# Gate and value products one pair ahead, tiles turned one by one, output sums in two halves

## The chip, the cores and the metric

One core of a Trainium2 chip runs the whole program once. The metric is the device time of one execution in microseconds (us). The kernel before took 796.15 us, median of three runs (794.65 to 797.71).

## The reference, cut to what matters

Three layers follow each other on 2304 tokens (4 batches of 576) with 512 features. First a windowed attention, then a mixture of 8 experts with one expert for each token (its result is x), then a gated layer:

```python
gate = 1.0 / (1.0 + np.exp(-(x @ w_gate)))      # w_gate, w_val: 512 x 1536
val = x @ w_val
return (gate * val @ w_out).astype(np.float32)  # w_out: 1536 x 512
```

## The kernel before, in words

The program runs attention, then the experts (`moe_phase`, line 1050), then the gated layer (`moe2_phase`, line 1289). The order of the instructions on every engine's queue is the order in which Python writes them: the schedule is by hand.

**Numbers in two parts.** A float32 operand of the expert's second product and of the gated layer is held as a high and a low part (hi, lo). A product of two such operands is three matmuls: high by high, high by low and low by high (`three`, line 923; `dots`, line 930). ScalarE makes the high part by a cast, VectorE the low part by a subtraction.

**The gated layer.** Its 1536 inner features are 12 chunks f of 128, in 6 pairs q. The tokens are 5 blocks b: block 0 has the tiles of 128 tokens 0 and 1, the blocks 1 to 4 have four tiles each (2 to 5, 6 to 9, 10 to 13, 14 to 17). `s1(f, b)` (line 1326) makes a chunk: `first_products` (line 1278) does the gate and the value product, 12 matmuls each, into two PSUM banks (for block 0 into two halves of one). Then ScalarE takes Tanh (L1341, th), VectorE multiplies (L1342), ScalarE casts the high part (L1345, gh), VectorE subtracts for the low part (L1346, gl). `s2(q, b, parts)` (line 1349) makes the output sums of a block: for every tile six matmuls into one of two banks (6, 7), and the sum is added to `acc` in SBUF, by ScalarE (L1359) at q = 0, by VectorE (L1361, fo) later. At q = 5 SP then stores the tile. `s2` of a block is put (`due`) behind the first `s1` of the next block, all its tiles in a row; for block 0 at q = 0 it stands ahead of block 1, and in the last block of q = 5 behind the second `s1`.

**The first block.** Block 0 is loaded and turned in the expert stage (`xo`, line 1215, `turn_old`, `add_last`, `first_xt`). There half of the products of chunks 0 and 1 are started (lines 1271 and 1274). The tiles 2 to 17 are loaded from DRAM on SP's queue (`load_x`, L1310, tile fx), four ahead, and turned by `make_xt` (line 1313): four transposes on TensorE (L1320), a cast on ScalarE (L1322, fxh), a subtraction on VectorE (L1323, fxl), then the next load. They follow the two chunks of block 0, 1, 2 and 3 at q = 0, two tiles behind each chunk. Tiles 2 and up of DRAM can be read once the last expert's results are scattered (L1084, POOL's queue).

**Weight conversion.** The gated layer's weights lie as 64-bit words in DRAM and are made into float32 parts on the way, in 36 halves of 512 columns (a weight chunk is two halves, a pair has three chunks: gate, value, out). `Convert.tick` (line 1042) moves each of six stages on by at most one half: l loads it raw (SP, L989, cv_raw, 512 KB), o subtracts for the low part (VectorE, L1009), h casts the high part (ScalarE, L1006), c multiplies by the sign (POOL, L999), b rebuilds the number (ScalarE L1032 for the sign, VectorE L1034, L1035, L1038), a takes the absolute value (ScalarE, L994). `until` bounds the casts, so that no part is written over one still in use; five weight chunks have room. In the expert stage `TICKS` says how many ticks follow each expert (11 in all), in the gated layer two ticks follow each chunk of a pair's first block and one each later chunk.

**An expert.** For each of the 8 experts four weight chunks: `products1` (L1157) into one of three banks, then ScalarE (L1202, hh) and VectorE (L1203, hl), `split` of a weight chunk (L919, L920) and `feed` (loads on SP, L910). Then the next expert's tokens are turned (`make_xt` of `moe_phase`), the ticks come, then the second products (L925 to L927), VectorE's `add_up` (L1183), and the scatters on POOL's queue.

Of the kernel before, what the change touches and what calls it, by code (L numbers as in the profile page):

```python
# [8 lines left out]
F32 = mybir.dt.float32  # L9
F32R = mybir.dt.float32r  # L10
BF16 = mybir.dt.bfloat16
I32 = mybir.dt.int32
ACTF = mybir.ActivationFunctionType
ALU = mybir.AluOpType
# [864 lines left out]
class Weights:  # L879
# [4 lines left out]
    N1, N2, NP, NX = 8, 6, 4, 4  # L884
# [38 lines left out]
def three(nc, out, lh, rh, first, last):  # L923

    nc.tensor.matmul(out, lhsT=lh[0], rhs=rh[0], start=first, stop=False)  # L925
    nc.tensor.matmul(out, lhsT=lh[0], rhs=rh[1], start=False, stop=False)  # L926
    nc.tensor.matmul(out, lhsT=lh[1], rhs=rh[0], start=False, stop=last)  # L927


def dots(nc, out, lh, rh, k0, k1, first, last):  # L930

    for k in range(k0, k1):
        for a in range(2):
            nc.tensor.matmul(  # L934
                out, lhsT=lh[a][:, k], rhs=rh[0][:, k], start=first and k + a == k0, stop=False,
                skip_group_check=True,
            )
    for k in range(k0, k1):
        nc.tensor.matmul(  # L939
            out, lhsT=lh[0][:, k], rhs=rh[1][:, k], start=False, stop=last and k == k1 - 1, skip_group_check=True  # L940
        )
# [108 lines left out]
def moe_phase(nc, tc, ctx, g, wt, pool_a, na, route, xd, cv, over, new_xt):  # L1050
# [1 line left out]

    TICKS = (0, 3, 3, 3, 2, 0, 0, 0)
    pool_b = ctx.enter_context(tc.tile_pool(name="m_w", bufs=1, reuse_waits="tile"))
    px = ctx.enter_context(tc.tile_pool(name="m_x", bufs=3, reuse_waits="tile"))
    p = ctx.enter_context(tc.tile_pool(name="m_p", bufs=2, reuse_waits="tile"))
# [30 lines left out]
    def make_xt(e):  # L1089
        xt = p.tile([128, 4, CAP], F32, tag="xt", name="xt")  # L1090

        def turn(h):
            for k in range(4):
                nc.tensor.transpose(xts[h][:, k], xg[e, h][:, 128 * k:128 * k + 128], g.ident)

        turn(0)
        nc.scalar.copy(out=xt[:, :, 0:128], in_=xts[0])
        if e == 0:
            load_n(0)
        with tc.If(taken[e] > 128) as c:  # L1100
            turn(1)
        with c.Else():
            nc.tensor.matmul(xts[1][:, 0, 0:32], lhsT=g.one, rhs=g.one[:, 0:32], start=True, stop=True)
        nc.vector.tensor_copy(xt[:, :, 128:256], xts[1])
        return xt
# [88 lines left out]
    xt = make_xt(0)  # L1194
    for e in range(E):
        hs = []
        for c in range(4):
            ps = g.bank()
            cases(taken[e], lambda n: products1(e, c, n), (128, 144, 160, 192, 256))
            hi = p.tile([128, 2, CAP], F32R, tag="hh", name="hh", bufs=5)  # L1200
            lo = p.tile([128, 2, CAP], F32R, tag="hl", name="hl", bufs=5)
            nc.scalar.activation(out=hi, in_=ps, func=ACTF.Relu)  # L1202
            nc.vector.scalar_tensor_tensor(  # L1203
                out=lo, in0=ps, scalar=0.0, in1=hi.bitcast(F32), op0=ALU.max, op1=ALU.subtract
# [7 lines left out]
            if c == 0 and e == E - 1:  # L1212
# [6 lines left out]
                for h in range(2):  # L1219
                    nc.gpsimd.tensor_scalar(  # L1220
                        out=hot[:, h], in0=route.iota, scalar1=to[:, h:h + 1], scalar2=None, op0=ALU.is_equal
# [3 lines left out]
        if e + 1 < E:  # L1225
            xt = make_xt(e + 1)
        for _ in range(TICKS[e]):
            cv.tick()
# [13 lines left out]
    t = p.tile([128, 4, CAP], F32R, tag="xt", name="part")  # L1242
# [26 lines left out]
    scatter(e, 0)  # L1269
    begun = [(t[:, 0], t[:, 1]) for t in (g.bank(), g.bank())]  # L1270
    first_products(nc, cv, begun[0], xt0, 0, 0, 2)
    add_last(0, 1)
    first_xt(1)
    first_products(nc, cv, begun[1], xt0, 1, 0, 2)
    return xt0, begun


def first_products(nc, cv, ps, xt, f, k0=0, k1=4):


    fs = slice(128 * (f % 2), 128 * (f % 2) + 128)
    shared = xt[0].shape[2] == 256
    for i in range(2):
        whi, wlo = cv.need(3 * (f // 2) + i, 4)
        first = k0 == 0 and (i == 0 or not shared)
        dots(nc, ps[i], (whi[:, :, fs], wlo[:, :, fs]), xt, k0, k1, first, k1 == 4)


def moe2_phase(nc, tc, ctx, g, cv, xt0, begun, acc, xd, out):


    KF = FF // 128
    NP, NB = KF // 2, 5
    tiles = [(0, 1)] + [tuple(range(4 * b - 2, 4 * b + 2)) for b in range(1, NB)]
    p = ctx.enter_context(tc.tile_pool(name="f_p", bufs=2, reuse_waits="tile"))
    px = ctx.enter_context(tc.tile_pool(name="f_xt", bufs=1, reuse_waits="tile"))
    xt = {0: xt0}
    for b in range(1, NB):
        xt[b] = tuple(px.tile([128, 4, 512], F32R, name=f"f{n}{b}") for n in ("xh", "xl"))
    pairs, sums, spares = [(3, 4), (5, 1)], (6, 7), (0, 2)  # L1300
    turn = {"s1": 0, "s2": 0, "x": 0}
    xn = {}

    def bank(i, n=512):
        return g.all[i][:, 0:n]

    def load_x(t):
        if t < NT // 128:
            x = p.tile([128, DM], F32, tag="x", name="fx", bufs=4)
            nc.sync.dma_start(out=x, in_=xd[128 * t:128 * t + 128, :])  # L1310
            xn[t] = x

    def make_xt(t):
        b, a = (t + 2) // 4, (t + 2) % 4
        hi, lo = xt[b]
        x = xn.pop(t)
        turn["x"] += 1
        ps = bank(spares[turn["x"] % 2]).rearrange("p (a c) -> p a c", c=128)
        for k in range(4):
            nc.tensor.transpose(ps[:, k], x[:, 128 * k:128 * k + 128], g.ident)  # L1320
        s = slice(128 * a, 128 * a + 128)
        nc.scalar.copy(out=hi[:, :, s], in_=ps)  # L1322
        nc.vector.tensor_tensor(out=lo[:, :, s], in0=ps, in1=hi[:, :, s].bitcast(F32), op=ALU.subtract)  # L1323
        load_x(t + 4)

    def s1(f, b):
        n = 128 * len(tiles[b])
        k0 = 2 * (b == 0 and f < 2)
        if k0:
            ps = begun[f]  # L1330
        else:
            pair = pairs[turn["s1"] % 2]
            turn["s1"] += 1
            if b == 0:
                ps = bank(pair[0]).rearrange("p (a c) -> p a c", c=256)
                ps = (ps[:, 0], ps[:, 1])
            else:
                ps = (bank(pair[0]), bank(pair[1]))
        first_products(nc, cv, ps, xt[b], f, k0)
        th = p.tile([128, n], F32, tag="th", name="th")  # L1340
        nc.scalar.activation(out=th, in_=ps[0], func=ACTF.Tanh, scale=0.5)  # L1341
        nc.vector.scalar_tensor_tensor(out=th, in0=th, scalar=1.0, in1=ps[1], op0=ALU.add, op1=ALU.mult)  # L1342
        hi = p.tile([128, n], F32R, tag="gh", name="gh", bufs=4)
        lo = p.tile([128, n], F32R, tag="gl", name="gl", bufs=4)
        nc.scalar.copy(out=hi, in_=th)  # L1345
        nc.vector.tensor_tensor(out=lo, in0=th, in1=hi.bitcast(F32), op=ALU.subtract)  # L1346
        return hi, lo

    def s2(q, b, parts):
        whi, wlo = cv.need(3 * q + 2, 2)  # L1350
        for a, t in enumerate(tiles[b]):
            ps = bank(sums[turn["s2"] % 2])
            turn["s2"] += 1
            s = slice(128 * a, 128 * a + 128)
            for i, (hi, lo) in enumerate(parts):
                three(nc, ps, (hi[:, s], lo[:, s]), (whi[:, i], wlo[:, i]), i == 0, i == 1)
            o = acc[t]
            if q == 0:
                nc.scalar.activation(out=o, in_=ps, func=ACTF.Copy, scale=0.5)  # L1359
            else:  # L1360
                nc.vector.scalar_tensor_tensor(out=o, in0=ps, scalar=0.5, in1=o, op0=ALU.mult, op1=ALU.add)  # L1361
            if q == NP - 1:
                nc.sync.dma_start(out=out[128 * t:128 * t + 128, :], in_=o)

    for t in range(2, 6):
        load_x(t)
    after = {(0, 0): (2, 3), (0, 1): (4, 5)}
    for b in range(1, NB - 1):
        after[b, 0], after[b, 1] = tuple(range(4 * b + 2, 4 * b + 4)), tuple(range(4 * b + 4, 4 * b + 6))
    due = None  # L1370
    for q in range(NP):
        order = list(range(NB)) if q < NP - 1 else [1, 2, 3, 4, 0]
        for b in order:
            if (q, b) == (0, 1):
                s2(*due)
                due = None
            parts = []
            last = q == NP - 1 and b == 0
            for i in range(2):
                parts.append(s1(2 * q + i, b))  # L1380
                if q == 0:
                    for t in after.get((b, i), ()):
                        make_xt(t)
                if due and i == last:
                    s2(*due)
                    due = None
                cv.until(2 * min(3 * q + 5, 3 * NP))
                for _ in range(1 + (b == order[0])):
                    cv.tick()
            due = (q, b, parts)  # L1390
    s2(*due)


class Overflow:
# [287 lines left out]
```

## Time and profile before

| what | value |
|---|---|
| median of three runs | 796.15 us (794.65 to 797.71) |
| the profiled execution | 798.2 us |
| its span, first to last instruction | 796.4 us |
| TensorE busy | 739.7 us (93% of the span) |
| VectorE, ScalarE, POOL busy | 421.4, 310.6, 141.1 us |
| mean granted TensorE clock | 0.968 of full speed |
| expert stage, about | 150 to 309.7 us |
| gated layer, about | 309.7 to 796 us |

PE is TensorE's matmuls, PEld its weight loads (which overlap), DVE is VectorE, ACT is ScalarE, SP and POOL are the engines whose queues issue the DMAs. PEclk is the granted clock as a share of the full 2.4 GHz. A matmul's time in a row includes the pipeline's length, so the distance between two starts is its cost. In a timeline row the numbers are the start in us, the length in us, engine, line and operation, output and input by the program's names, the shape and the count; what stands in brackets is how long the engine was idle before it and what ended that. A row by stretch has the stretch, its length, the busy us (and count) of PE, PEld, DVE, ACT and POOL, the granted clock, the mean busy share of the 16 DMA engines and GB/s.

### The profile page before, as it was taken

What the parts mean: (1) busy time and instruction counts of PE and PEld (TensorE: products, weight loads), DVE (VectorE), ACT (ScalarE), POOL (GpSimd) and SP (SyncE); (2) the same over time, 40 slices, a digit from 0 to 9 for tenths busy, and PEclk for the clock granted to TensorE, in tenths of its full rate; (3) what the DMA queues carried; (4) which work ended last, traced back from release to release, by engine and by line L of the source; (5) the groups of instructions that cost most, each with busy time, mean ns of one, the idle gap of its engine ahead of it and who ended that gap; (6) DMA issues with size and microseconds to landing.
All of it is one profiled execution on the core that took longest, in us unless ns stands there. A gap on an engine that the chain in (4) does not pass through costs nothing.

```text
span 796.4 us, 13025 instructions
## 1 busy us (share of the span) xinstructions
PE 739.7 (93%) x4976; PEld 594.0 (75%) x4976; DVE 421.4 (53%) x880; ACT 310.6 (39%) x677; POOL 141.1 (18%) x163
## 2 busy tenths in 40 slices
PE   6989989689998798799999999999999999999995
PEld 3656665478997798677787788778877887777784
DVE  8568677548857564622146336543653473333232
ACT  5887885235544453433253114312431151111110
POOL 7223333312433232200011101100210020000000
PEclk7799999889999999999999999999999999999998
DMA  7779879696697723510002101210220000001112
GB/s 158 170 174 215 219 154 310 183 352 209 201 323 261 271 92 116 181 54 28 0 27 80 53 0 54 67 39 1 56 77 26 1 27 0 1 1 53 54 54 84
DMA packets 74999, 88.13 MB, mean 111 GB/s; under 512 B 15810, under 2 KB 52930, under 8 KB 74912
## 3 DMA queue, kind: packets, MB, share of 16 engines
q1 hardware_dynamic: 71008, 78.68, 34.0%
q0 software_dynamic: 2560, 6.15, 2.3%
q10 hardware_dynamic: 1344, 2.10, 0.7%
q8 instruction: 60, 0.98, 0.5%
q14 instruction: 27, 0.22, 0.1%
HBM read 75.52 MB, written 13.63 MB: 112 GB/s over the span
## 4 chain that ended last, share of the span: by engine, by line
PE 78%; ACT 8%; DVE 6%; DMA 4%; issue 2%; DVEq 0%; SPq 0%; ACTq 0%
PE bank L934 25%; PE bank L939 12%; PE bank L925 9%; PE bank L927 8%; PE bank L926 8%; PE bank L1157 7%; ACT kTd L237 2%; DMA cv_raw<-in_moe_w_out_dram 2%; ACT qTd L237 1%; PE ps_s L255 1%; PE ps_t L221 1%; ACT p L269 1%; ACT kTp L237 1%; ACT xt L386 1%; PE ps_o L302 1%
## 5 line engine op out<-in xcount | busy, mean ns | idle before, releaser
L934 PE MATMUL bank<-fxh,w_hi 128*128 128x512 f32 (+1 forms) x480 | 176.6, 374 | 4.8 <-ACT fxh L1322 4.8
L934 PE MATMUL bank<-fxh,w_lo 128*128 128x512 f32 (+1 forms) x480 | 175.2, 371 | 0.0
L1342 DVE SCALAR_TENSOR_TENSOR th<-th,bank 128x512 f32<-128x512 f32 (+1 forms) x60 | 38.0, 634 | 185.9 <-PE bank L939 168.9
L939 PE MATMUL bank<-fxl,w_hi 128*128 128x512 f32 (+1 forms) x480 | 121.1, 372 | 0.0
L934 PEld LDWEIGHTS bank<-fxh,w_hi 128*128 128x128 f32 x480 | 90.5, 188 | 23.1 <-ACT fxh L1322 5.5
L999 POOL TENSOR_TENSOR cv_x<-cv_x,cv_s 128x512 f32<-128x512 f32 x36 | 48.8, 1357 | 320.2 <-DVE cv_x L1038 320.0
L934 PEld LDWEIGHTS bank<-fxh,w_lo 128*128 128x128 f32 x480 | 90.5, 189 | 16.7
L939 PEld LDWEIGHTS bank<-fxl,w_hi 128*128 128x128 f32 x480 | 85.7, 189 | 17.1
L925 PE MATMUL bank<-w_hi,gh 128*128 128x512 f32 x216 | 87.9, 407 | 5.0 <-ACT gh L1345 4.5
L1341 ACT ACTIVATE th<-bank 128x512 f32<-128x512 f32 (+1 forms) x60 | 33.1, 552 | 146.4 <-PE bank L939 146.4
L1345 ACT CAST gh<-th 128x512 fp32r<-128x512 f32 (+1 forms) x60 | 34.7, 578 | 140.5 <-DVE th L1342 140.5
L927 PE MATMUL bank<-w_hi,gl 128*128 128x512 f32 x216 | 86.0, 398 | 0.0
L926 PE MATMUL bank<-w_lo,gh 128*128 128x512 f32 x216 | 85.9, 397 | 0.0
L1157 PE MATMUL bank<-xt,w 128*128 128x128 f32 (+3 forms) x512 | 72.3, 304 | 13.7 <-issue 8.2
L1157 PEld LDWEIGHTS bank<-xt,w 128*128 128x128 f32 x512 | 70.1, 207 | 16.0 <-issue 9.1
L1361 DVE SCALAR_TENSOR_TENSOR fo<-bank,fo 128x512 f32<-128x512 f32 x90 | 61.7, 688 | 37.0 <-PE bank L927 36.0
L1346 DVE TENSOR_TENSOR gl<-th,gh 128x512 fp32r<-128x512 f32 (+1 forms) x60 | 38.9, 649 | 38.6 <-ACT gh L1345 38.6
L925 PEld LDWEIGHTS bank<-w_hi,gh 128*128 128x128 f32 x216 | 40.9, 189 | 21.4 <-DVE fo L1361 7.6
L927 PEld LDWEIGHTS bank<-w_hi,gl 128*128 128x128 f32 x216 | 41.1, 190 | 10.2 <-DVE gl L1346 0.5
L926 PEld LDWEIGHTS bank<-w_lo,gh 128*128 128x128 f32 x216 | 41.1, 190 | 8.4
L994 ACT ACTIVATE cv_x<-cv_raw 128x512 f32<-128x512 f32 x36 | 24.3, 675 | 57.0 <-issue 24.0
L920 DVE TENSOR_TENSOR w_lo<-w,w_hi 128x1024 fp32r<-128x1024 f32 x32 | 39.1, 1222 | 4.2 <-ACT w_hi L919 4.0
(215 smaller groups left out, 1059.6 us busy)
## 6 DMA issues: line engine op xcount, KB each, us to landing
w<-in_moe_w_dram SPq DMA_DIRECT2D x62, 512.0 KB
cv_raw<-in_moe_w_val_dram SPq DMA_DIRECT2D x12, 512.0 KB
cv_raw<-in_moe_w_out_dram SPq DMA_DIRECT2D x12, 512.0 KB
cv_raw<-in_moe_w_gate_dram SPq DMA_DIRECT2D x10, 512.0 KB
out_dram<-fo SPq DMA_DIRECT2D x18, 256.0 KB
fx<-xd SPq DMA_DIRECT2D x16, 256.0 KB
kp<-in_k_dram SPq DMA_DIRECT2D x12, 192.0 KB
qp<-in_q_dram SPq DMA_DIRECT2D x12, 192.0 KB
```

Of the source, the lines that this page charges most:

```text
L920: self.nc.vector.tensor_tensor(out=lo, in0=raw, in1=hi.bitcast(F32), op=ALU.subtract)
L925: nc.tensor.matmul(out, lhsT=lh[0], rhs=rh[0], start=first, stop=False)
L926: nc.tensor.matmul(out, lhsT=lh[0], rhs=rh[1], start=False, stop=False)
L927: nc.tensor.matmul(out, lhsT=lh[1], rhs=rh[0], start=False, stop=last)
L934: nc.tensor.matmul(out, lhsT=lh[a][:, k], rhs=rh[0][:, k], start=first and k + a == k0, stop=False, skip_group_check=True,)
L939: nc.tensor.matmul(out, lhsT=lh[0][:, k], rhs=rh[1][:, k], start=False, stop=last and k == k1 - 1, skip_group_check=True)
L999: nc.gpsimd.tensor_tensor(out=self.x[i], in0=self.x[i], in1=self.s.pop(i), op=ALU.mult)
L1157: nc.tensor.matmul(ps[:, a, 0:n], lhsT=wt.one[4 * e + c][:, k, 128 * a:128 * a + 128], rhs=xt[:, k, 0:n], start=(k == 0), stop=(k == 3),)
L1342: nc.vector.scalar_tensor_tensor(out=th, in0=th, scalar=1.0, in1=ps[1], op0=ALU.add, op1=ALU.mult)
L1345: nc.scalar.copy(out=hi, in_=th)
L1346: nc.vector.tensor_tensor(out=lo, in0=th, in1=hi.bitcast(F32), op=ALU.subtract)
L1361: nc.vector.scalar_tensor_tensor(out=o, in0=ps, scalar=0.5, in1=o, op0=ALU.mult, op1=ALU.add)
```

## The change

`TICKS` goes from 11 to 15 ticks: one fewer after expert 1, one more after expert 4, two each after experts 5 and 6. With that the first five weight chunks are converted before the gated layer starts. There, the two chunks of pair 1 for block 0 (`ahead`) are computed right behind those of pair 0, before block 0's first sums; they keep their own buffers until pair 1, which then has no block 0 of its own. `make_xt` is called between the gate and the value product of a chunk (`between`), one tile at a time. `s2` becomes a list of one call for each tile (`sums_of`): two sums follow a block's first chunk, the rest the second. At pair 0 there are no ticks until block 3; later pairs have three ticks ahead of their first block and one behind each chunk. The bank pairs change places and th has one buffer.

```diff
-    TICKS = (0, 3, 3, 3, 2, 0, 0, 0)
+    TICKS = (0, 2, 3, 3, 3, 2, 2, 0)
...
-def first_products(nc, cv, ps, xt, f, k0=0, k1=4):
+def first_products(nc, cv, ps, xt, f, k0=0, k1=4, between=None):
...
         dots(nc, ps[i], (whi[:, :, fs], wlo[:, :, fs]), xt, k0, k1, first, k1 == 4)
+        if between:
+            between()
...
-    pairs, sums, spares = [(3, 4), (5, 1)], (6, 7), (0, 2)
+    pairs, sums, spares = [(5, 1), (3, 4)], (6, 7), (0, 2)
     turn = {"s1": 0, "s2": 0, "x": 0}
-    xn = {}
+    xn, todo, due = {}, [], []
...
+    def between():
+        if todo:
+            todo.pop(0)()
...
-        first_products(nc, cv, ps, xt[b], f, k0)
-        th = p.tile([128, n], F32, tag="th", name="th")
+        first_products(nc, cv, ps, xt[b], f, k0, between=None if k0 else between)
+        z, bufs = ("0", 2) if b == 0 and f // 2 == 1 else ("", 4)
+        hi, lo = (p.tile([128, n if z else 512], F32R, tag=t + z, name=t, bufs=bufs)[:, 0:n] for t in ("gh", "gl"))
+        th = p.tile([128, 512], F32, tag="th", name="th", bufs=1)[:, 0:n]
         nc.scalar.activation(out=th, in_=ps[0], func=ACTF.Tanh, scale=0.5)
         nc.vector.scalar_tensor_tensor(out=th, in0=th, scalar=1.0, in1=ps[1], op0=ALU.add, op1=ALU.mult)
-        hi = p.tile([128, n], F32R, tag="gh", name="gh", bufs=4)
-        lo = p.tile([128, n], F32R, tag="gl", name="gl", bufs=4)
...
-    def s2(q, b, parts):
+    def s2(q, a, t, parts):
         whi, wlo = cv.need(3 * q + 2, 2)
-        for a, t in enumerate(tiles[b]):
...
+    def sums_of(q, b, parts):
+        return [lambda a=a, t=t: s2(q, a, t, parts) for a, t in enumerate(tiles[b])]
+
+    def flush(left=0):
+        while len(due) > left:
+            due.pop(0)()
 
     for t in range(2, 6):
         load_x(t)
-    after = {(0, 0): (2, 3), (0, 1): (4, 5)}
-    for b in range(1, NB - 1):
-        after[b, 0], after[b, 1] = tuple(range(4 * b + 2, 4 * b + 4)), tuple(range(4 * b + 4, 4 * b + 6))
-    due = None
+    due += sums_of(0, 0, [s1(0, 0), s1(1, 0)])
+    todo += [lambda: None] + [lambda t=t: make_xt(t) for t in range(2, 6)]
+    ahead = [s1(2, 0), s1(3, 0)]
+    while due:
+        due.pop(0)()
+        between()
     for q in range(NP):
-        order = list(range(NB)) if q < NP - 1 else [1, 2, 3, 4, 0]
+        if q == 1:
+            due += sums_of(1, 0, ahead)
+        order = list(range(1, NB)) if q < 2 else [1, 2, 3, 4, 0] if q == NP - 1 else list(range(NB))
         for b in order:
-            if (q, b) == (0, 1):
-                s2(*due)
-                due = None
+            first = b == order[0]
+            cv.until(2 * min(3 * q + (4 if first else 5), 3 * NP))
+            if q and first:
+                for _ in range(3):
+                    cv.tick()
+            if q == 0 and b < NB - 1:
+                todo += [lambda t=t: make_xt(t) for t in range(4 * b + 2, 4 * b + 6)]
             parts = []
-            last = q == NP - 1 and b == 0
             for i in range(2):
                 parts.append(s1(2 * q + i, b))
-                if q == 0:
-                    for t in after.get((b, i), ()):
-                        make_xt(t)
-                if due and i == last:
-                    s2(*due)
-                    due = None
-                cv.until(2 * min(3 * q + 5, 3 * NP))
-                for _ in range(1 + (b == order[0])):
+                if i and todo:
+                    between()
+                flush(0 if i else 2)
+                if q or b > 2:
                     cv.tick()
-            due = (q, b, parts)
-    s2(*due)
+            due += sums_of(q, b, parts)
+    flush()
```

## Rows read from the trace of the kernel before

**Rows 1.** Busy time by stretch: us, then each engine's busy us (count), clock, DMA.

```profile
309.70:326.66 16.96, 9.74 (x54) 7.76 (x53) 11.58 (x21) 8.80 (x17) 4.07 (x3) 0.90 0.71 226
...
398.83:786.00 387.17, 386.62 (x1760) 313.00 (x1759) 175.27 (x282) 99.47 (x175) 29.53 (x22) 1.00 0.12 37
```

**Rows 2.** Timeline of TensorE, start of the gated layer.

```profile
309.71 0.28 PE L934 MATMUL bank<-fxh,w_hi 128*128 128x256 f32 x1
...
314.03 1.32 PE L1320 MATMUL bank<-ident,fx 128*128 128x128 f32 x8 [2.71 <-DMA fx<-xd]
...
322.83 0.71 PE L925 MATMUL bank<-w_hi,gh 128*128 128x512 f32 x1 [4.49 <-ACT gh L1345]
...
326.66 0.39 PE L934 MATMUL bank<-fxh,w_hi 128*128 128x512 f32 x1
```

**Rows 3.** Chain of waits through the two holes: start, us, what.

```profile
311.29 2.69 DMA fx<-xd
...
316.70 0.60 DVE w_lo L1009
...
322.01 0.34 DVE th L1342
```

**Rows 4.** Chain of waits at block 1's last tiles, and in sums at q = 0.

```profile
338.96 0.70 DVE th L1342
...
340.29 0.98 ACT fxh L1322 x2
...
387.84 0.23 PE bank L925
```

**Rows 5.** Waits from 296 us on: who, for whom, total us, times, longest.

```profile
PEld bank L925 <- DVE fo L1361: 7.6, 16, 0.5
...
PE bank L934 <- ACT fxh L1322: 4.8, 3, 1.6
```

**Rows 6.** Timeline of TensorE behind transposes, and within four sums.

```profile
333.03 0.48 PE L934 MATMUL bank<-fxh,w_hi 128*128 128x512 f32 x1
...
449.33 0.40 PE L927 MATMUL bank<-w_hi,gl 128*128 128x512 f32 x1
449.77 0.50 PE L925 MATMUL bank<-w_hi,gh 128*128 128x512 f32 x1
```

**Rows 7.** Timeline of ScalarE in the expert stage.

```profile
262.27 0.66 ACT L994 ACTIVATE cv_x<-cv_raw 128x512 f32<-128x512 f32 x1 [5.21 <-DMA cv_raw<-in_moe_w_out_dram]
...
283.30 0.60 ACT L1202 ACTIVATE hh<-bank 128x512 fp32r<-128x512 f32 x1 [0.84 <-PE bank L1157]
```

**Rows 8.** Timeline of SP's queue in the expert stage.

```profile
250.20 1.12 SPq L989 DMA_DIRECT2D cv_raw<-in_moe_w_out_dram  x2
...
298.23 1.33 SPq L1215 DMA_DIRECT2D xo<-xd  x2
```

**Rows 9.** Timeline of TensorE in the expert stage.

```profile
241.84 2.44 PE L1157 MATMUL bank<-xt,w 128*128 128x160 f32 x16 [1.96 <-DVE hl L1203]
...
255.57 1.95 PE L1157 MATMUL bank<-xt,w 128*128 128x128 f32 x16
...
264.20 3.16 PE L1157 MATMUL bank<-xt,w 128*128 128x128 f32 x16 [2.07 <-DVE hl L1203]
...
303.36 0.60 PE L1124 MATMUL bank<-ident,xo 128*128 128x128 f32 x4
```

**Rows 10.** Busy time by stretch in the expert stage: columns as in rows 1.

```profile
265.00:270.00 5.00, 5.00 (x26) 4.63 (x25) 5.00 (x7) 4.23 (x6) 1.00 (x1) 0.67 0.57 167
270.00:275.00 5.00, 5.00 (x29) 4.33 (x28) 2.81 (x4) 0.00 (x0) 2.05 (x2) 1.00 1.08 397
```

**Rows 11.** Timeline of VectorE in the expert stage.

```profile
248.63 0.68 DVE L1009 TENSOR_TENSOR w_lo<-cv_x,w_hi 128x512 fp32r<-128x512 f32 x1
...
250.76 0.69 DVE L1009 TENSOR_TENSOR w_lo<-cv_x,w_hi 128x512 fp32r<-128x512 f32 x1
...
288.39 0.74 DVE L1183 SCALAR_TENSOR_TENSOR xg<-bank,r_gslot,xg 128x512 f32<-128x512 f32 x1
```

More of the change, by code (lines that the diff above doesn't have):

```diff
@@ L1347, in s1 @@
         return hi, lo
-    def s2(q, b, parts):
+    def s2(q, a, t, parts):
         whi, wlo = cv.need(3 * q + 2, 2)
-        for a, t in enumerate(tiles[b]):
[L1352 to L1357, printed above, removed]
-            if q == 0:
[L1359 to L1363, printed above, removed]
+        ps = bank(sums[turn["s2"] % 2])
+        turn["s2"] += 1
+        s = slice(128 * a, 128 * a + 128)
+        for i, (hi, lo) in enumerate(parts):
+            three(nc, ps, (hi[:, s], lo[:, s]), (whi[:, i], wlo[:, i]), i == 0, i == 1)
+        o = acc[t]
+        if q == 0:
+            nc.scalar.activation(out=o, in_=ps, func=ACTF.Copy, scale=0.5)
+        else:
+            nc.vector.scalar_tensor_tensor(out=o, in0=ps, scalar=0.5, in1=o, op0=ALU.mult, op1=ALU.add)
+        if q == NP - 1:
+            nc.sync.dma_start(out=out[128 * t:128 * t + 128, :], in_=o)
@@ L1377, in moe2_phase @@
             parts = []
-            last = q == NP - 1 and b == 0
             for i in range(2):
                 parts.append(s1(2 * q + i, b))
-                if q == 0:
-                    for t in after.get((b, i), ()):
-                        make_xt(t)
-                if due and i == last:
-                    s2(*due)
-                    due = None
-                cv.until(2 * min(3 * q + 5, 3 * NP))
-                for _ in range(1 + (b == order[0])):
+                if i and todo:
+                    between()
```

## The prediction, made before the change was built

> **What bounds the kernel now.** I read the busy shares by stage first, then TensorE's timeline for its holes, then the chain of waits through each hole, then the other engines where the change puts work. The reader should see that the second half of the kernel (gate, value and output products, from 309.7 us on) is TensorE's own time with few holes. From 398.83 to 786.00 TensorE is busy 386.62 of 387.17 us at full granted clock, while VectorE is busy 175 and ScalarE 99 [rows 1]: only fewer or shorter holes can shorten this stretch. From 309.70 to 326.66 it is busy 9.74 of 16.96 us at a granted clock of 0.90 [rows 1]. There the holes are.
>
> The first hole, 2.71 us, ends with the load of the first x tile (fx). The second, 4.49 us, ends with ScalarE's gh; behind it the products take 0.71 us instead of about 0.4 [rows 2]. The chain shows why. The x tile cannot be read before the last scatter is done, and lands 2.69 us after its issue. And gh of the second chunk waited for VectorE, which from 316.70 to 322.01 worked only on weight conversions (L1009, L1034 to L1038) queued ahead of L1342 [rows 3]: the order of the program was late there, not the engine.
>
> **The change part by part.** The sum is made against the profiled execution, 798.2 us with a span of 796.4; the median of the three runs shown is 796.15, 2 us lower, and I take the saving off that median.
>
> *Start of the second stage.* A 128x512 product takes 0.23 us from start to start [rows 4], a 128x256 one half of that, 0.12. The stretch from 309.71 to 326.66 [rows 2] holds 24 products of 256 columns (2.9 us), 16 transposes (about 1.6) and 12 products of 512 (2.8): 7.3 of 16.95 us. So 9.6 us are lost. After the change the two chunks of the second pair (48 products of 256, 5.7 us, only moved here from a later place) stand between the first pair and the sums. The first x tile is then wanted at 309.71 + 2.9 + 2.9 = 315.5, 1.5 us after it lands (311.29 + 2.69) [rows 3], and gh of the second chunk only at about 320. With no conversions queued ahead it is ready some 2.2 us after its products: a chain as at 338.96, where L1342 takes 0.70 us and L1345 and L1346 about as long [rows 4]. Both holes go, and the slow clock with them: I take 9.4 us, leaving 0.2 for switching. If x came over 1.5 us later than now, the 2.71 us hole would come back from that point on.
>
> *Tiles turned one by one.* TensorE waits three times for fxh, 4.8 us in all [rows 5]: two tiles are turned after a chunk's products, and their two casts (0.98 us) stand on ScalarE behind that chunk's L1342 and L1345 [rows 4]. After the change a tile's cast is issued ahead of its chunk's Tanh, so it waits for nothing but its own transposes. Before the second and third of these places two sums (12 products, 2.8 us) stand between the last tile and its use, which hides a cast of 0.5 to 0.6 us. At the first place nothing is due, and a wait of about 0.8 us stays. The product behind transposes takes 0.48 us, not 0.39 [rows 6]; 8 more such switches cost 8 x 0.09 = 0.7. So 4.8 - 0.8 - 0.7 = 3.3 us are saved.
>
> *Sums in two halves.* Four sums in a row use two banks, so the third waits until VectorE has read the first (L1361), behind the chunk's L1346. The wait list has 16 such waits [rows 5]. One costs: 449.33 to 449.77 is 0.44 us instead of 0.23, and the next product takes 0.11 longer [rows 6], 0.32 together; 16 x 0.32 = 5.1 us. Two sums at a time have two banks, and 5.6 us of products pass before the next two: the wait goes wholly. In the last block two sums still stand behind the last chunk, 2.8 us, and cover its chain, so the tail behind the last product stays.
>
> *Conversions left out of pair 0, and three ticks at each later pair's start.* Per tick VectorE has 2.13 us (248.63 to 250.76) [rows 11] and ScalarE three operations. By the code only chunks of weights whose old slot is done are written there. A pair has 387.17 / 5 = 77 us of products [rows 1] against 13 ticks, so TensorE does not wait for them: nothing, covered by the products; if ScalarE were late by more than the 5.6 us of one chunk, the bank pair would be late by the excess. The single buffer of th is a rival below.
>
> *Ticks moved into the expert stage* (15 for 11: one fewer at expert 1, one more at 4, two each at 5 and 6). This is the price. At expert 4 ScalarE stood 5.21 us for a raw weight that was issued at 250.20 and landed at 262.27 [rows 7, 8], 12 us, since the DMA engines are full (share 1.08 [rows 10]). The next chunk's activation stood behind it, and TensorE waited 2.07 us for hl; its next 16 products took 3.16 us, where 16 such took 1.95 [rows 9]. A third tick there waits for a second raw half, 0.5 MB at the 397 GB/s of that time [rows 10] or 1.3 us later, and VectorE's part of it stands in front of that activation's partner: 1.3 + 1.0 = 2.3 us. At expert 5 a new wait of the same kind: the raw half is issued behind eight weight loads (4.2 MB, 10.6 us at that rate, from about 272 on with the shift of 2.3), so it lands about 284 as an estimate, and hl follows some 2.4 us later; TensorE wants that bank when the third chunk is done, 283.2 by ScalarE's row at 283.30 [rows 7], plus the 2.3: about 1.0 us. At expert 6 two ticks hold VectorE about 4 us ahead of L1183 (now at 288.39 [rows 11]), and with it the two scatters in POOL's queue and SP's load of xo behind them, now issued at 298.23 for transposes at 303.36 [rows 8, 9]. Some 3.5 us fit in between without loss; I count 1.0. On SP's queue the four loads stand behind the chunk's own weights and put off only loads wanted an expert later. Together 4.3 us. Ends: nothing, if ScalarE has caught up each time before its bank is wanted; and the 5.21 us of the row for each of two new bursts, some 10 us.
>
> The sum: 9.4 + 3.3 + 5.1 - 4.3 = 13.5 us. 796.15 - 13.5 = **782.6 us** (span about 783).
>
> *A rule weighed.* After the wait of 2.07 us the granted clock was 0.67 over 265 to 270 us [rows 10], a mean of its levels 1.2 and 2.4 GHz: TensorE idled and then ran part of the time at half rate. The Trainium skill ("TensorE: Matmul & The Clock Gate", section HAM oscillation) says that a product stage with repeated idle gaps pays for the return to full clock each time, which speaks against bursts of ticks in a stage that has such gaps already. By the row alone my 4.3 holds only waits; by the rule the waits at experts 5 and 6 would each bring a slow stretch, as in rival 2.
>
> **The rivals.** (1) *The moved ticks cost nothing.* For it: behind the old burst of three ticks at expert 3 TensorE waited 1.96 us and no more [rows 9]. Against it: the 5.21 us row. Time 796.15 - 17.8 = 778.4. (2) *Each moved burst costs a full wait and a slow stretch.* At experts 5 and 6 a wait of 2.07 and 3.16 - 1.95 = 1.21 us for the clock, instead of 1.0: 2 x 2.3 = 4.6 us more, and 1.2 more at expert 4. Time 782.6 + 5.8 = 788.4. For it: the clock row; against it: at expert 6 no raw weight is awaited. (3) *Slower: the single buffer of th.* Tanh of the next chunk may not start until L1346 of this one is done. The chain is about 2.2 us and the next first product ends 2.8 us after it starts, so 0.6 us is left; beyond that the bank pair is late only once the delay exceeds a further 2.8 us. Should VectorE's sums (L1361) and conversions push it past that in every chunk, each of 48 wide chunks would lose about one L1342, 0.70 us: 34 us, 782.6 + 34 = 816. It decides only if the chain grows by over 3 us; VectorE at 175 of 387 us speaks against that. That the holes stay because x lands late is inside the forecast's spread: 2.7 us.
>
> **How the numbers follow.** Forecast 0.60, rival 1 0.20, rival 2 0.15, rival 3 0.05. The range runs from rival 1 less 2 us of spread between runs to rival 2 plus 2: 776.5 to 790.5; it leaves out rival 3 and parts of the edges. Half a per cent, 4.0 us, is about what a measurement of this kernel can tell from no change; it lies at 792.2. Faster: nearly all of forecast and rival 1, and half of rival 2 or more, 0.86. Within half a per cent: the rest, 0.09. Slower: 0.05, rival 3.
>
> **What the changed profile would show.** No wait of TensorE over 1 us between the first product of the second stage and the last; granted clock 1.00 from there on; the 16 waits for L1361 gone; one wait for fxh of about 0.8 us in place of three of 1.6. In the expert stage: ScalarE's waits for cv_raw at experts 4 and 5, holes of TensorE for hl of some 4 us at 262 and 1 us near 285, xo issued some 3 us later against the products around it. I am wrong if the second stage, first to last product, shrinks by less than 14 us; if the expert stage grows by over 10 us; or if Tanh (L1341) is seen waiting for L1346 with TensorE idle.

## The result and the profile after

The changed kernel took 783.24 us (median of four runs, 781.82 to 786.3), the kernel before beside it 795.4 us: ratio 0.9839, 95% interval 0.9809 to 0.9869. The forecast was 782.6 us. The profiled execution took 786.3 us with a span of 784.6, 11.8 us below that of before (796.4). Both profiled executions are slower than their kernels' medians, by 2.8 us before and 3.1 after.

The gain is a difference of two numbers. The gated layer, from its first product to the start of its last, took 786.97 - 309.71 = 477.26 us before and takes 775.84 - 317.12 = 458.72 us now: 18.5 us less. But it starts 7.4 us later, since the expert stage grew; the rest, 0.7 us, lies behind the last product.

TensorE by stretch after the change, columns as in [rows 1]: the start of the gated layer up to the first product of block 1, and all the rest of it.

```profile
317.12:330.36 13.24, 13.24 (x103) 12.41 (x101) 5.37 (x13) 5.60 (x13) 1.23 (x1) 1.00 0.53 155
330.36:775.84 445.48, 444.81 (x2028) 363.21 (x2028) 187.47 (x306) 120.56 (x211) 28.43 (x22) 1.00 0.12 39
```

Both holes of [rows 1] and [rows 2] are gone: TensorE is busy 13.24 of 13.24 us at full clock, and 5.74 us of these are the pair that was moved here (48 products of 256 columns, 0.12 us each). So the start gained 16.95 - (13.24 - 5.74) = 9.45 us. The timeline of TensorE shows the first x tile turned without a wait, and the one wait for a cast that is left; the wait list from 296 us on has nothing of L1367 (L1361 before) any more, and one wait for fxh for the three of [rows 5].

```profile
322.88 0.60 PE L1323 MATMUL bank<-ident,fx 128*128 128x128 f32 x4
...
344.20 0.50 PE L934 MATMUL bank<-fxh,w_hi 128*128 128x512 f32 x1 [0.67 <-ACT fxh L1325]
```

```profile
PE bank L934 <- ACT fxh L1325: 0.7, 1, 0.7
```

In the expert stage TensorE's timeline shows the price. The rows are the first products of the experts 5, 6 and 7, and one second product of expert 6; they answer to [rows 9].

```profile
265.15 2.63 PE L1157 MATMUL bank<-xt,w 128*128 128x128 f32 x16 [3.31 <-DVE hl L1203]
...
279.18 5.13 PE L1157 MATMUL bank<-xt,w 128*128 128x128 f32 x29 [2.51 <-DMA w<-in_moe_w_dram]
...
286.35 2.05 PE L1157 MATMUL bank<-xt,w 128*128 128x128 f32 x16 [1.20 <-DVE hl L1203]
...
292.85 0.50 PE L926 MATMUL bank<-w_lo,hh 128*128 128x512 f32 x1 [0.86 <-DVE w_lo L920]
...
302.84 2.05 PE L1157 MATMUL bank<-xt,w 128*128 128x128 f32 x16 [1.45 <-DVE hl L1203]
```

ScalarE's timeline has the two waits for a raw weight behind the first two of the waits for hl, as [rows 7] had one:

```profile
260.86 0.67 ACT L994 ACTIVATE cv_x<-cv_raw 128x512 f32<-128x512 f32 x1 [4.80 <-DMA cv_raw<-in_moe_w_val_dram]
...
284.42 0.67 ACT L994 ACTIVATE cv_x<-cv_raw 128x512 f32<-128x512 f32 x1 [4.11 <-DMA cv_raw<-in_moe_w_gate_dram]
```

The last one, at expert 7, has another cause. VectorE's timeline shows a weight's low part of expert 6 stretched to 2.78 us (the others of that line take 1.2, but for one of 1.93), then the two ticks of expert 6, then `add_up` at 299.65, 11 us later than in [rows 11], and only at 302.10 the hl of expert 7's first chunk, for whose bank TensorE waited.

```profile
290.01 2.78 DVE L920 TENSOR_TENSOR w_lo<-w,w_hi 128x1024 fp32r<-128x1024 f32 x1
...
299.65 1.40 DVE L1183 SCALAR_TENSOR_TENSOR xg<-bank,r_gslot,xg 128x512 f32<-128x512 f32 x2
...
302.10 0.69 DVE L1203 SCALAR_TENSOR_TENSOR hl<-bank,hh 128x512 fp32r<-128x512 f32 x1
```

### The profile page after: what moved, and what is told of

Same layout as the page of the kernel before. It is cut to its first block, busy times and chain, and to the rows that moved or that the text cites. A ratio compares the mean times of both kernels' runs of the same rounds, so it can differ in the third digit from the quotient of the medians.

```text
span 784.6 us, 13023 instructions
## 1 busy us (share of the span) xinstructions
PE 733.7 (94%) x4976; PEld 592.3 (75%) x4976; DVE 417.3 (53%) x880; ACT 310.4 (40%) x677; POOL 141.2 (18%) x163
## 4 chain that ended last, share of the span: by engine, by line
PE 77%; DVE 8%; ACT 7%; DMA 4%; issue 3%; POOL 0%; SPq 0%; DVEq 0%; ACTq 0%; POOLq 0%
PE bank L934 26%; PE bank L939 13%; PE bank L927 8%; PE bank L926 8%; PE bank L925 8%; PE bank L1157 5%; DVE w_lo L920 2%; DMA cv_raw<-in_moe_w_val_dram 2%; ACT kTd L237 2%; DMA cv_raw<-in_moe_w_gate_dram 2%; ACT qTd L237 1%; PE ps_s L255 1%; PE ps_o L302 1%; DVE hl L1203 1%; ACT xt L386 1%
## 5 line engine op out<-in xcount | busy, mean ns | idle before, releaser
L999 POOL TENSOR_TENSOR cv_x<-cv_x,cv_s 128x512 f32<-128x512 f32 x36 | 47.7, 1327 | 307.4 <-ACT cv_x L994 168.7
L925 PE MATMUL bank<-w_hi,gh 128*128 128x512 f32 x216 | 85.6, 396 | 0.0
L1367 DVE SCALAR_TENSOR_TENSOR fo<-bank,fo 128x512 f32<-128x512 f32 x90 | 61.5, 686 | 5.1 <-PE bank L927 2.9
L1353 DVE TENSOR_TENSOR gl<-th,gh 128x512 fp32r<-128x512 f32 (+1 forms) x60 | 39.1, 652 | 38.7 <-ACT gh L1352 38.7
L920 DVE TENSOR_TENSOR w_lo<-w,w_hi 128x1024 fp32r<-128x1024 f32 x32 | 41.3, 1291 | 3.7 <-ACT w_hi L919 3.4
```

The source lines that it names most:

```text
L920: self.nc.vector.tensor_tensor(out=lo, in0=raw, in1=hi.bitcast(F32), op=ALU.subtract)
L999: nc.gpsimd.tensor_tensor(out=self.x[i], in0=self.x[i], in1=self.s.pop(i), op=ALU.mult)
```

## The experiments

Theory: the new order of the gated layer gains some 18 us, and the ticks moved into the expert stage give a part of it back. The rivals say that the ticks cost nothing, or that another part of the change does the work. This table holds what TensorE's timeline gave in the one profiled execution of each run, in us; the third column is the time from the last 16 of expert 4's first products (241.84 in [rows 9], "expert 4's row" below) to the gated layer's first product, free of what happened earlier. The ratio is of medians, against the kernel before run beside it. The three kernels whose gated layer is that of the changed kernel gave 458.7 us each time, while the start of the layer moved by 5 us among them: where no slow stretch falls into it, a difference of 1 us in the length can be read; one in the start hardly.

| kernel | ticks | expert 4 to gated layer | gated layer starts | its length | ratio to before (95% interval) |
|---|---|---|---|---|---|
| before | 11 | 67.9 | 309.7 | 477.3 | |
| changed | 15 | 75.8 | 317.1 | 458.7 | 0.9839 (0.9809, 0.9869) |
| ticks alone | 15 | 74.4 | 315.6 | 472.1 | 0.9997 (0.9969, 1.0024) |
| no pair ahead | 15 | 75.1 | 316.9 | 463.1 | 0.9921 (0.9897, 0.9944) |
| four sums in a row | 15 | 75.0 | 316.4 | 474.3 | 1.0023 (0.9994, 1.0053) |
| two tiles at a time | 15 | 74.7 | 317.0 | 459.8 | 0.9885 (0.9833, 0.9936) |
| changed, again | 15 | 74.2 | 312.4 | 458.7 | 0.9856 (0.9824, 0.9887) |
| none at expert 6 | 14 | 72.0 | 313.2 | 458.7 | 0.9799 (0.9741, 0.9857) |
| old ticks, no pair ahead | 11 | 65.9 | 307.8 | 461.5 | 0.9793 (0.9745, 0.9841) |
| ten ticks, no pair ahead | 10 | 64.4 | 306.1 | 461.8 | 0.9816 (0.9766, 0.9867) |
| the same, again | 10 | 64.7 | 307.9 | 462.7 | 0.9793 (0.9763, 0.9822) |
| ten ticks, filled hole | 10 | 65.3 | 305.2 | 461.9 | 0.9787 (0.9736, 0.9837) |
| eight ticks | 8 | 62.6 | 301.4 | 465.9 | 0.9796 (0.9762, 0.9829) |

**Ticks alone**, in the kernel before:

```diff
-    TICKS = (0, 3, 3, 3, 2, 0, 0, 0)
+    TICKS = (0, 2, 3, 3, 3, 2, 2, 0)
```

> The kernel before with the new TICKS (15) and nothing else. Theory (the moved ticks cost time in the expert stage, and the conversions queued on VectorE made the second hole): the gated layer starts 4 to 8 us later than the 309.7 us of before; in it the second hole (4.5 us and the slow products behind it, about 6 us in all) is gone, the hole for the x tile (2.7 us) and the waits for fxh and L1361 stay; so the time is within 3 us of the kernel before. Rival (the moved ticks cost nothing, the 7.4 us later start of the changed kernel is spread between runs): start near 309.7 us and 6 us faster.

Measured: 797.73 us, no change; start 5.9 us later, the layer 5.1 us shorter. The waits of TensorE from 296 us on:

```profile
PEld bank L925 <- DVE fo L1361: 7.5, 16, 0.5
PEld bank L934 <- ACT fxh L1322: 5.5, 3, 1.8
PE bank L934 <- ACT fxh L1322: 4.8, 3, 1.6
...
PE bank L1320 <- DMA fx<-xd: 2.5, 1, 2.5
```

All waits of before stand there but the one for gh. So the second hole was the conversions on VectorE, and they can be had out of its way without any new order; and moving them costs as much as that hole did. The rival falls.

**No pair ahead**, in the changed kernel:

```diff
-    todo += [lambda: None] + [lambda t=t: make_xt(t) for t in range(2, 6)]
-    ahead = [s1(2, 0), s1(3, 0)]
-    while due:
-        due.pop(0)()
-        between()
+    for t in range(2, 6):
+        make_xt(t)
+    flush()
...
-        if q == 1:
-            due += sums_of(1, 0, ahead)
-        order = list(range(1, NB)) if q < 2 else [1, 2, 3, 4, 0] if q == NP - 1 else list(range(NB))
+        order = list(range(1, NB)) if q == 0 else [1, 2, 3, 4, 0] if q == NP - 1 else list(range(NB))
```

> The changed kernel without the pair ahead: block 0 of pair 1 comes in its own place, the four first tiles are turned behind the second chunk. Theory (conversions out of the way do most of it, the pair ahead only fills the wait for the x tile): a hole of 1.4 to 2.7 us before the first transposes, no wait for gh, 1.5 to 3 us slower than the changed kernel. Rival (the pair ahead is what removed both holes): 9 us slower than the changed kernel.

Measured: the layer 4.4 us longer, half of what the rival wanted, more than the theory's 3. TensorE's timeline:

```profile
321.19 1.38 PE L1323 MATMUL bank<-ident,fx 128*128 128x128 f32 x8 [1.25 <-DMA fx<-xd]
323.73 1.94 PE L1323 MATMUL bank<-ident,fx 128*128 128x128 f32 x8 [1.16 <-DMA fx<-xd]
325.32 0.78 PE L925 MATMUL bank<-w_hi,gh 128*128 128x512 f32 x1
325.89 0.63 PE L926 MATMUL bank<-w_lo,gh 128*128 128x512 f32 x1
```

No wait for gh; two waits for x tiles, 2.4 us, and behind them slow products (0.63 for about 0.4): the granted clock was 0.56 from 325 to 327 us. So the pair ahead is worth the x wait and the clock that follows it, not both holes. Where no slow stretch follows, it is worth less: with the old ticks, below, x waits of 1.15, 0.20 and 0.69 us left the clock at 1.00, and the layer was 2.8 us longer than the changed kernel's.

**Four sums in a row**, in the changed kernel:

```diff
-                flush(0 if i else 2)
+                if i or not (q == NP - 1 and b == 0):
+                    flush()
```

> The changed kernel with all sums of a block in a row behind the next block's first chunk, as before. Theory: the 16 waits for L1361 come back at 0.32 us each, 5 us slower than the changed kernel, and the wait list shows some 16 of them. Rival (one tile less in the queue of VectorE, so the waits were hidden by the new order of ticks): within 1 us of the changed kernel.

Measured: the layer 15.6 us longer, three times the theory's 5; the whole gain of the change is gone. The wait list, then VectorE and TensorE around one of three long waits:

```profile
PEld bank L925 <- DVE fo L1367: 14.7, 19, 2.6
PE bank L925 <- DVE fo L1367: 6.0, 3, 2.2
...
PE bank L934 <- ACT fxh L1325: 2.0, 3, 0.7
```

```profile
473.41 1.29 DVE L1009 TENSOR_TENSOR w_lo<-cv_x,w_hi 128x512 fp32r<-128x512 f32 x2
474.84 0.43 DVE L1034 TENSOR_SCALAR cv_x<-cv_x 128x512 f32<-128x512 f32 x1
...
478.10 1.27 DVE L1367 SCALAR_TENSOR_TENSOR fo<-bank,fo 128x512 f32<-128x512 f32 x2
```

```profile
478.83 0.50 PE L925 MATMUL bank<-w_hi,gh 128*128 128x512 f32 x1 [1.87 <-DVE fo L1367]
```

The 16 short waits are back, as the theory said. New are three waits of about 2 us: the three ticks that now stand ahead of a pair's first block hold VectorE from 473.41 on, and L1367 comes only behind them. One of the three, of 2.22 us, was followed by a slow stretch; the other two, of 1.87 us, were not:

```profile
638.00:641.00 3.00, 3.00 (x10) 2.43 (x10) 1.13 (x2) 0.00 (x0) 0.00 (x0) 0.50 0.00 0
```

And all three waits for fxh are back, if shorter than before. So the halves carry two other parts: they make the bursts of ticks harmless, and they cover the last tile's cast.

**Two tiles at a time**, in the changed kernel:

```diff
-        first_products(nc, cv, ps, xt[b], f, k0, between=None if k0 else between)
+        first_products(nc, cv, ps, xt[b], f, k0, between=between if b == 0 and not k0 else None)
...
-                if i and todo:
-                    between()
+                if q == 0:
+                    for _ in range(2):
+                        between()
```

> The changed kernel with two tiles turned behind each chunk of blocks 1 to 3, as before, and the sums still in halves. Theory (two sums behind the last tiles hide the casts at blocks 2 and 3 either way, so turning one by one is worth little beside the halves): one wait for fxh of about 1.6 us instead of 0.7, eight fewer switches at 0.09 us, so the gated layer within 0.5 us of the changed kernel. Rival (turning one by one saves the 3.3 us that the prediction gave it): three waits, 3 us slower.

Measured: the layer 1.0 us longer. The wait list has one wait, longer than the changed kernel's 0.7:

```profile
PE bank L934 <- ACT fxh L1325: 1.6, 1, 1.6
```

The theory, at most 0.5 us, was short by half a microsecond; the rival's three waits do not come. Turning one by one is worth 1.0 us once the sums are halved.

**Old ticks, and none at expert 6.** The first is made from the kernel with no pair ahead:

```diff
-    TICKS = (0, 2, 3, 3, 3, 2, 2, 0)
+    TICKS = (0, 3, 3, 3, 2, 0, 0, 0)
...
-                if q or b > 2:
+                if q or b > 0:
```

> The changed kernel without the pair ahead, with the old 11 ticks in the expert stage, and its conversions of the gated layer begun behind block 1 instead of block 3. Theory (the 15 ticks put off the start of the gated layer by 6 to 7 us): start near 309.7 us, the gated layer about 463 us as in the run without the pair ahead, 4 us faster than the changed kernel, near 779 us. Rival (the start near 317 us has another cause than the ticks, or the conversions made up later hold the first blocks): start near 316 us or new waits for gh in blocks 1 and 2, no faster than the run without the pair ahead, 789 us.

The second is the changed kernel with one line of its own:

```diff
-    TICKS = (0, 2, 3, 3, 3, 2, 2, 0)
+    TICKS = (0, 3, 3, 3, 3, 2, 0, 0)
```

> The changed kernel with 14 ticks: three after expert 1 again, none after expert 6. Theory (the two ticks at expert 6 hold VectorE and POOL ahead of the last expert): the waits for w_lo near 292 and for hl near 301 go, the gated layer starts about 3 us earlier than in the changed kernel, 3 us faster. Rival (all the delay comes from the loads at experts 4 and 5): the same start within 1 us, the same time.

Measured: with the old ticks the layer starts at 307.8 us, and takes 461.5; with none at expert 6 the start is 313.2. Three timelines of TensorE, the first products that waited: old ticks,

```profile
241.90 2.44 PE L1157 MATMUL bank<-xt,w 128*128 128x160 f32 x16 [1.83 <-DVE hl L1203]
...
263.63 2.02 PE L1157 MATMUL bank<-xt,w 128*128 128x128 f32 x16 [1.76 <-issue]
...
280.32 2.02 PE L1157 MATMUL bank<-xt,w 128*128 128x128 f32 x16 [0.29 <-issue]
```

none at expert 6 (the 64 products of expert 7 run without a wait),

```profile
263.54 2.76 PE L1157 MATMUL bank<-xt,w 128*128 128x128 f32 x16 [2.40 <-DMA w<-in_moe_w_dram]
...
284.91 3.58 PE L1157 MATMUL bank<-xt,w 128*128 128x128 f32 x16 [2.21 <-DVE hl L1203]
294.48 7.31 PE L1157 MATMUL bank<-xt,w 128*128 128x128 f32 x64
```

and the changed kernel once more, in a run of its own:

```profile
238.22 2.44 PE L1157 MATMUL bank<-xt,w 128*128 128x160 f32 x16 [0.58 <-DVE hl L1203]
...
261.40 2.95 PE L1157 MATMUL bank<-xt,w 128*128 128x128 f32 x16 [3.15 <-DVE hl L1203]
...
274.23 3.50 PE L1157 MATMUL bank<-xt,w 128*128 128x128 f32 x29 [1.31 <-issue]
279.84 0.49 PE L1157 MATMUL bank<-xt,w 128*128 128x128 f32 x3 [2.11 <-issue]
281.59 2.05 PE L1157 MATMUL bank<-xt,w 128*128 128x128 f32 x16 [1.26 <-DVE hl L1203]
...
298.08 2.05 PE L1157 MATMUL bank<-xt,w 128*128 128x128 f32 x16 [1.45 <-DVE hl L1203]
```

The kernel before has the old ticks too. Its last 16 of expert 6's first products stand at the end of a longer row:

```profile
277.80 7.25 PE L1157 MATMUL bank<-xt,w 128*128 128x128 f32 x48 [2.07 <-issue]
...
283.10 1.95 PE L1157 MATMUL bank<-xt,w 128*128 128x128 f32 x16
```

From one expert's last 16 first products to the next's, in us:

| kernel | expert 4 to 5 | 5 to 6 | 6 to gated layer |
|---|---|---|---|
| before (11 ticks, none at 5 and 6) | 22.4 | 18.9 | 26.6 |
| old ticks, no pair ahead (the same 11) | 21.7 | 16.7 | 27.5 |
| six profiles with 15 ticks | 22.8 to 24.1 | 20.2 to 21.2 | 30.8 each |
| none at expert 6 | 22.3 | 21.4 | 28.3 |

By the means, the third tick at expert 4 costs 1.4 us, the two at expert 5 2.8 and the two at expert 6 3.7. The second is the least sure, since the two kernels with 11 ticks differ there by 2.2 us. The third is 2.5 by the run without those ticks, in which the 16 products at 284.91 ran slow (3.58 us for 2.05). Both theories hold for the waits and, counted from expert 4's row, for the starts. That these two kernels are faster than the changed one by the 4 and 3 us expected is not shown: their medians are 781.23 and 782.75 us for its 783.24, and their intervals overlap that of the changed kernel.

**Ten ticks; ten ticks and a filled hole.** Both start from the kernel with old ticks and no pair ahead:

```diff
-    TICKS = (0, 3, 3, 3, 2, 0, 0, 0)
+    TICKS = (0, 3, 3, 3, 1, 0, 0, 0)
```

and the second also has products of ones into a bank that is free then, whose sums nobody reads:

```diff
+    fill = bank(1).rearrange("p (a c) -> p a c", c=128)
     for t in range(2, 6):
+        if t % 2 == 0:
+            for _ in range(5):
+                g.ones(fill)
         make_xt(t)
```

> As the run with the old ticks, with one tick instead of two after expert 4 (10 in all, just what block 0 needs). Theory (ScalarE's wait for a raw weight in the second tick there causes the wait for hl at 262 us and the slow clock behind it): both go, the gated layer starts 2 to 4 us earlier than with 11 ticks. Rival (TensorE waits there for the weights of the expert itself, the full DMA engines being the limit): the same start within 1 us, the wait being taken over by the weight loads.

> As the run with 10 ticks, with five products of ones, 512 columns each, in front of the first and of the third of the first four tiles, while TensorE waits for the x tiles (the result of these products is not used). Theory (TensorE is idle for the x tiles there anyway, and the idle time brings the slow clock behind it): the products of the first sums run at 0.23 us again, 1.5 to 2 us faster than without them. Rival (the clock falls for another reason, or the tiles come in time): the same or 2 us slower.

Measured: start at 306.1 us, 1.7 earlier than with 11 ticks; from expert 4's row 64.4 for 65.9 us. That is just under the 2 to 4 us of the theory: the wait behind expert 4 shrank, it did not go (1.17 us at 263.15, for 1.76). In time nothing was gained over 11 ticks, 781.73 us for 781.23. The filled hole brought nothing, 461.9 for 461.8 us: in the run without the filling the clock had not fallen, 1.00 from 310 to 315 us, and its 10 products took the place of the wait:

```profile
308.09 1.25 PE L1611 MATMUL bank<-r_one 128*128 128x512 bf16 x5
309.55 1.37 PE L1323 MATMUL bank<-ident,fx 128*128 128x128 f32 x8 [0.21 <-DMA fx<-xd]
310.75 1.24 PE L1611 MATMUL bank<-r_one 128*128 128x512 bf16 x5
```

**The changed kernel and ten ticks side by side, and eight ticks.** The last is made from the kernel with ten:

```diff
-    TICKS = (0, 3, 3, 3, 1, 0, 0, 0)
+    TICKS = (0, 3, 3, 2, 0, 0, 0, 0)
...
         make_xt(t)
-    flush()
...
-                flush(0 if i else 2)
+                if q or b > 1:
+                    flush(0 if i else 2)
```

> The changed kernel once more, on the chip of the next two, so that they can be compared with it. Theory (the start of the gated layer hangs on the ticks and not on the run): start at 315 to 318 us, the gated layer 458.7 us, ratio near 0.984. Rival (the later start is spread): start anywhere from 306 to 318 us.

> The kernel with 10 ticks and no pair ahead once more. Theory: start near 306 us, the gated layer 461.8 us, so 5 to 8 us faster than the changed kernel on this chip. Rival (the start moves with the run): no difference beyond the interval.

> As the kernel with 10 ticks, with 8 ticks in the expert stage (two after expert 3, none after 4); the first sums, which need the two ticks left out, come behind block 2's first chunk. Theory (each burst put off costs the expert stage): start 1 to 3 us earlier than with 10 ticks, the gated layer about 1 us longer, since nothing covers the cast of the last tile of block 1; together 1 us faster to 1 us slower. Rival (expert 4 has no wait left that a tick makes): the same start, 1 us slower.

Measured, side by side: 783.77 us for the changed kernel, 779.61 for ten ticks, 778.84 for eight. The intervals of the first two do not overlap, 0.9824 to 0.9887 and 0.9763 to 0.9822: ten ticks without the pair ahead beat the changed kernel by some 4 us (0.5%), less than the 5 to 8 expected, and the kernel before by 16. The start of the changed kernel was 312.4 us here, outside the 315 to 318 of the theory, as the rival had it: some 3 us of spread lie ahead of expert 4 (its row is at 238.22 for 241.3), and the time from there is 74.2 us, close to the 74.4 to 75.8 of the others with 15 ticks. With eight ticks the time from expert 4's row is some 2 us shorter than with ten, but the layer is 3 to 4 us longer instead of 1, as the waits at its start, now uncovered, brought the slow clock: no gain.

```profile
310.00:315.00 5.00, 4.33 (x12) 3.14 (x11) 1.05 (x2) 0.58 (x1) 0.00 (x0) 0.54 0.41 112
```

## Why the prediction was right

**The start of the gated layer** was forecast at 9.4 us and gave 9.45. Its reason holds, and the runs split it: conversions out of the way about 5 us, the pair ahead 4.4 (2.8 where no slow stretch followed the x waits).

**Tiles one by one (3.3) and sums in halves (5.1)** were forecast at 8.4 us together and gave 18.54 - 9.45 = 9.1. The step that hides the casts behind two sums was right, and it was booked under the wrong edit: by the run with two tiles at a time, turning one by one is worth 1.0 us, and without the halves the layer loses 15.6. The 0.32 us for each of 16 waits fits: of the 15.6, the three long waits take 6.0, the waits for fxh 1.3 more than in the changed kernel and the slow stretch some 1.7, which leaves about 0.4 for each short one. What was missed is that the third ticks at a pair's start would have made three waits of 2 us, had the halves not been there; I had costed those ticks at nothing, with the products as cover, and the cover is the halves.

**The ticks moved into the expert stage** were forecast at 4.3 us: 2.3 at expert 4, 1.0 at 5, 1.0 at 6. This is the term that was mis-sized. The start moved by 7.4 us in the profiles; from expert 4's row on it is 74.9 us (mean of six profiles with 15 ticks) against 66.9 (two with 11), so 8.0 us: 1.4, 2.8 and 3.7 by expert.

At expert 4 the estimate was high, but its reason holds, a row of ScalarE that stands for a raw half (4.80 us at 260.86). The DMA share of 1.08 and the 397 GB/s that it quotes are those of 270 to 275 us; while the raw half of [rows 7] was on its way, from 250.20 to 262.27 us, they were 1.01 and 366.

At expert 5 the place and the reason were right: the raw half landed at 284.42 us, estimated for about 284, and TensorE started expert 6's last first products at 286.35. The six other profiles with ticks at expert 5 show the same 1.9 us between the two. In the changed kernel's second profile it is 281.59 less 279.66:

```profile
279.66 0.67 ACT L994 ACTIVATE cv_x<-cv_raw 128x512 f32<-128x512 f32 x1 [3.09 <-DMA cv_raw<-in_moe_w_gate_dram]
```

Rival 2 wanted a slow stretch as a further price there, and there is one: 29 products took 5.13 us at 279.18, where the second profile's 29 took 3.50 at full clock. But it cost next to nothing. In the second profile TensorE stood 2.11 us ahead of the next three products instead, and from expert 5 to 6 it is 20.2 us there and 21.2 here, each set by the landing. And the kernel before had such a stretch at the same products, with no tick behind expert 5. TensorE by stretch, before, and then after for the 1.02 us from the end of the wait and the 3 us that follow:

```profile
278.60:282.00 3.40, 3.40 (x19) 3.40 (x18) 0.44 (x1) 1.07 (x2) 0.30 (x1) 0.50 0.70 254
```

```profile
279.18:280.20 1.02, 1.02 (x8) 1.02 (x9) 0.00 (x0) 1.02 (x2) 1.02 (x1) 0.95 1.06 389
280.20:283.20 3.00, 3.00 (x16) 3.00 (x15) 0.00 (x0) 0.12 (x1) 0.11 (x1) 0.50 0.98 361
```

The Trainium skill ("TensorE: Matmul & The Clock Gate", HAM oscillation) tells of a wait for a load in which the clock falls, so that the products behind it start at half speed. This trace agrees in part: the wait of 2.51 us was for a load and half speed came behind it, but the first products still ran at a granted clock of 0.95.

At expert 6 the step named the wrong wait, and this is the larger miss. xo was issued at 306.90 us and turned at 310.77 without a wait (3.9 us ahead, for 5.1 before). VectorE itself came late: TensorE waited for a weight's low part (1.02 us lost at 292.85), for expert 7's hl at 302.84 (1.45 us), and for hl again among expert 7's second products, which take 6.0 us for 5.2. All six profiles with these two ticks have 30.8 us here, and the run without them has 28.3. So in size the prices at experts 5 and 6 come near rival 2's (3.3 us each); what made them is longer waits, not the clock.

**The sum** came out near since 18.5 + 0.7 - 7.4 = 11.8 us is not far from 13.5: the layer gained 0.7 more than forecast and the tail 0.7 (not looked into), the ticks took 3 more. That the medians came within 1 us of the forecast is in part luck, as errors of opposite sign met a spread of 4.5 us among the four runs. Rival 1 (ticks cost nothing) falls with the run of the ticks alone. Rival 3 (one buffer of th) did not show: ScalarE's timeline has one wait of Tanh for L1353 (L1346 before), among the chunks of block 0, and TensorE stood still only for fxh, 0.67 us, from the first product to the last.

```profile
320.65 0.38 ACT L1350 ACTIVATE th<-bank 128x256 f32<-128x256 f32 x1 [0.55 <-DVE gl L1353]
```

## What to carry to other kernels

Work that sits in an engine's queue ahead of what the critical engine waits for can be put off as well as done sooner: here putting the conversions off cost nothing and doing them sooner cost 8 us, about half of it behind loads while the DMA engines were full (a share of 1.05 to 1.08 from 274 to 281 us) and half on VectorE. An edit that moves work to fill a hole is worth the hole, less what the moved work needs earlier: the pair ahead gained 2.8 to 4.4 us and forced four ticks that cost more. And take the parts of a change out one at a time: the halves looked like 5 us and, in the new order, carried 15.

## What the runs showed of the hardware

A wait of much the same length is sometimes followed by the slow clock and sometimes not. With ten ticks the x tiles brought waits of 1.31, 0.30 and 0.56 us and the clock stayed at 1.00; in the second run of the same kernel waits of 1.06 and 0.62 us were followed by a stretch at 0.76, and the layer took 0.9 us longer:

```profile
310.00:315.00 5.00, 3.19 (x20) 2.30 (x19) 2.77 (x6) 2.36 (x6) 0.00 (x0) 0.90 0.78 261
315.00:320.00 5.00, 4.84 (x19) 3.96 (x19) 1.69 (x3) 2.00 (x4) 0.00 (x0) 0.76 0.57 159
```

And VectorE's L920, 1.2 us otherwise, took 2.78 from 290.01 on, while POOL multiplied one of the added halves:

```profile
290.37 1.33 POOL L999 TENSOR_TENSOR cv_x<-cv_x,cv_s 128x512 f32<-128x512 f32 x1
```

The two are linked. Over all 13 profiles L920 stands 416 times: of the 15 that ran beside an L999 of POOL 14 took 1.92 to 2.78 us, and of the other 401 none took over 1.4. In the one exception, with eight ticks, POOL began 0.90 us into L920 and was itself the longer one, 1.49 us for about 1.3. The 2.8 us come back in all six profiles with ticks at expert 6, and not in the run without them: some 1.6 us of what those two ticks cost.
